# Retention, routed experts and a dense MLP: token rows turned by VectorE in 32x32 blocks instead of by TensorE

## The chip, the cores and the metric

The kernel runs on one core of a Trainium2 chip, in one launch. The metric is the device time of that launch in microseconds (us). Engines are named as the profile names them: PE is TensorE's matmuls and PEld its weight loads, DVE is VectorE, ACT ScalarE, POOL GpSimd, and SP the engine that issues most transfers. Each engine works through its own queue in program order.

## The reference

All inputs and outputs are fp32; the kernel has to keep fp32's precision.

```python
# 1: retention attention, 8 batches, 8 heads, 576 positions, 64 features
scores = scale * np.matmul(q, k.transpose(0, 1, 3, 2))
out = np.matmul(scores * Dmat[None], v)           # Dmat: decay by head, causal
x = out.transpose(0, 2, 1, 3).reshape(4608, 512)
# 2: each token goes to one of 8 experts
logits = x @ w_gate + modality_bias[modality_id]
e_idx = np.argmax(logits, axis=1)                 # gate_w: the softmax value there
h = np.maximum(x[mask] @ w1[e], 0.0)              # w1: 512 x 1024 for each expert
out[mask] = gate_w[mask, None] * (h @ w2[e])      # w2: 1024 x 512
# 3: dense MLP, 512 -> 2048 -> 512
h = x @ w_in
return (h - np.tanh(h)) @ w_out
```

## The kernel before

Three stages follow each other: attention and routing (up to about 161 us in the profile), the experts (to 609 us) and the dense MLP (to the end). An fp32 product is made of three matmuls: each operand is split into a high part, rounded to a format in which PE runs at full rate (a cast on ACT), and a low part, the rest (a subtraction on DVE); high x high, low x high and high x low are summed in PSUM.

**Expert units.** Routing sorts the tokens by expert into units of 400 (UE) of one expert each; twelve units are always run, u = 0 to 11. A unit has eight steps, f = 0 to 7, one for each 128 of the expert's 1024 hidden features. `blocks` (L647) writes the program: in step i come gemm1 (12 matmuls at L661, into the PSUM tile `hp`), then `post`, then `prep`, then gemm2 of the step two before (12 matmuls, L863 to L865, into four `acc` tiles of 128x400). At f=1 gemm2 finishes the unit before, and `finish` copies its four `acc` tiles to `yo`: two on ACT (L842), two on DVE (L840). The next gemm2, at f=2, starts the tiles anew, so it has to wait for these copies.

**post.** Relu on ACT gives `hi` (L760) and DVE gives `lo` (L761). Then the 512 columns of w2 for step i-1 and the 512 of w1 for step i+2 are each split: cast L736 on ACT, subtraction L737 on DVE. A transfer on SP's queue loads the step's weights for the next unit (`raw`).

**prep.** The rows of unit u+1 come from DRAM with four indirect transfers on POOL (L156), 128 rows of 512 floats each. They have tokens on the partitions, and gemm1 needs features there: at f=3 to 6 `turn_rows` has PE transpose one row tile in four pieces of 128x128 (L146) into an `hp` tile, ACT casts it (`xh`, L147) and DVE subtracts (`xl`, L148). For unit 1, this is done at (0,6) and (0,7); a pair (u,f) stands for step f of unit u.

**Conversion pieces.** The third stage's weights, stored as 64-bit floats, are converted to fp32 and split during the experts: 32 conversions of 128x512 (`conv`), each cut into four pieces: L174 to L177, then L181, then L185 and L186 with the cast L187 on ACT, then L191, all else on DVE. `prep` takes two pieces at even f and one at odd f from a list.

Around this, in code that is printed here:

Of the kernel before, what the change touches and what calls it, by code (L numbers as in the profile page):

```python
# [50 lines left out]


# [941 lines left out]
```

## Time and profile before

| | |
|---|---|
| median of 3 runs (lowest, highest) | 1391.44 us (1391.1, 1391.64) |
| the profiled execution, and its span | 1399.9 us, 1398.2 us |
| mean granted clock of PE | 0.998 |
| busy: PE, PEld, DVE, ACT, POOL | 99%, 86%, 75%, 50%, 16% |
| first and last matmul of gemm1 in the experts | 161.1 us, 600.5 us |
| first matmul of the dense MLP | 608.9 us |

The profiled execution is one of its own and is some 8 us longer than the runs without a profile. Busy shares are over the whole span. Times in the rows below are microseconds from the span's start, unless marked ns.

### The profile page before, as it was taken

Reading aid. Unit: us, or ns where it says so; the run is one execution under the profiler, and the core shown is the slowest. Engines: PE = TensorE matmul, PEld = TensorE weight load, DVE = VectorE, ACT = ScalarE, POOL = GpSimd, SP = SyncE. Lnnn points to the kernel's source line nnn. Section 1 sums busy time; section 2 is a strip of 40 time slices with the busy share of each in tenths; the row PEclk is TensorE's granted clock in tenths of the full one; section 3 lists DMA queues with packets and bytes.
Section 4 is the critical chain, followed back from the end, with each engine's and each line's share of the span. In section 5 each row is a group of like instructions: output and inputs, shape, how many; then the busy total and the mean of one; then the engine's idle time right before and its main releaser. Section 6 shows DMA issues by size and latency. Waiting matters only on the chain.

```text
span 1398.2 us, 22551 instructions
## 1 busy us (share of the span) xinstructions
PE 1377.8 (99%) x8427; PEld 1204.7 (86%) x8427; DVE 1045.4 (75%) x1762; ACT 693.6 (50%) x1302; POOL 220.9 (16%) x290
## 2 busy tenths in 40 slices
PE   8999899999999999999999999999999999999998
PEld 7887699999999999988888888888888888888886
DVE  5766578888888888658877777787787877778775
ACT  3323344444444444446656555565555655555553
POOL 4555320111111111010111100111001110011101
PEclk9999999999999999999999999999999999999999
DMA  9997444554854436434000000000000000000000
GB/s 369 407 338 271 149 143 138 138 126 124 222 140 93 93 86 168 123 129 153 31 31 31 31 1 30 31 31 31 1 30 31 31 31 0 31 31 0 31 0 31
DMA packets 65266, 136.50 MB, mean 98 GB/s; under 512 B 22656, under 2 KB 29376, under 8 KB 65152
## 3 DMA queue, kind: packets, MB, share of 16 engines
q1 hardware_dynamic: 50368, 96.77, 23.1%
q0 software_dynamic: 7296, 19.57, 4.1%
q10 hardware_dynamic: 7488, 18.67, 3.5%
q8 instruction: 68, 1.11, 0.3%
q14 instruction: 46, 0.38, 0.1%
HBM read 132.95 MB, written 39.80 MB: 124 GB/s over the span
## 4 chain that ended last, share of the span: by engine, by line
PE 51%; issue 5%; POOL 0%; POOLq 0%; ACT 0%; DVE 0%
PE hp L661 26%; PE acc L940 8%; PE acc L938 8%; PE acc L939 8%; POOL out_dram L964 0%; POOLq L990 0%; ACT o L961 0%; POOL nopt L963 0%; POOLq L954 0%; DVE epsb L969 0%; POOLq L964 0%; DVE epsb L968 0%
## 5 line engine op out<-in xcount | busy, mean ns | idle before, releaser
L911 ACT ACTIVATE eh<-hp 128x512 f32<-128x512 f32 x144 | 86.4, 600 | 294.7 <-PE hp L661 269.6
L661 PE MATMUL hp<-xh,winh 128*128 128x512 f32 x576 | 224.1, 389 | 1.6 <-DVE epsb L969 1.6
L938 PE MATMUL acc<-wout,hi 128*128 128x512 f32 x576 | 224.2, 389 | 0.0
L940 PE MATMUL acc<-wout,lo 128*128 128x512 f32 x576 | 224.2, 389 | 0.0
L939 PE MATMUL acc<-wout,hi 128*128 128x512 f32 x576 | 224.1, 389 | 0.0
L661 PE MATMUL hp<-xl,winh 128*128 128x512 f32 x576 | 224.1, 389 | 0.0
L661 PE MATMUL hp<-xh,winl 128*128 128x512 f32 x576 | 224.1, 389 | 0.0
L913 DVE TENSOR_TENSOR el<-eh,hp 128x512 f32<-128x512 f32 x144 | 99.1, 688 | 152.3 <-ACT eh L912 151.3
L922 DVE SCALAR_TENSOR_TENSOR el<-eh,el 128x512 f32<-128x512 f32 x144 | 128.5, 893 | 15.4 <-issue 0.5
L863 PE MATMUL acc<-hi,wh 128*128 128x400 f32 x384 | 136.1, 354 | 0.2
L661 PE MATMUL hp<-xh,wh 128*128 128x400 f32 x384 | 132.0, 344 | 1.8 <-ACT wh L736 1.8
L661 PE MATMUL hp<-xl,wh 128*128 128x400 f32 x384 | 131.7, 343 | 0.5 <-DVE xl L148 0.5
L661 PE MATMUL hp<-xh,wl 128*128 128x400 f32 x384 | 131.9, 343 | 0.1
L864 PE MATMUL acc<-lo,wh 128*128 128x400 f32 x384 | 131.4, 342 | 0.0
L865 PE MATMUL acc<-hi,wl 128*128 128x400 f32 x384 | 131.4, 342 | 0.0
L661 PEld LDWEIGHTS hp<-xh,winh 128*128 128x128 f32 x576 | 108.0, 188 | 24.1 <-PEq L884 1.9
L760 ACT ACTIVATE hi<-hp 128x400 fp32r<-128x400 f32 x96 | 48.5, 505 | 161.0 <-PE hp L661 161.0
L938 PEld LDWEIGHTS acc<-wout,hi 128*128 128x128 f32 x576 | 108.2, 188 | 22.8 <-ACT hi L916 0.4
L940 PEld LDWEIGHTS acc<-wout,lo 128*128 128x128 f32 x576 | 108.1, 188 | 22.9 <-DVE lo L917 0.4
L661 PEld LDWEIGHTS hp<-xl,winh 128*128 128x128 f32 x576 | 108.1, 188 | 22.6
L661 PEld LDWEIGHTS hp<-xh,winl 128*128 128x128 f32 x576 | 108.1, 188 | 22.4
L939 PEld LDWEIGHTS acc<-wout,hi 128*128 128x128 f32 x576 | 108.1, 188 | 22.4
(166 smaller groups left out, 2529.0 us busy)
## 6 DMA issues: line engine op xcount, KB each, us to landing
raw<-in_w_dram SPq DMA_DIRECT2D x91, 512.0 KB
qk<-in_qk_dram SPq DMA_DIRECT2D x36, 512.0 KB
vk<-in_vk_dram SPq DMA_DIRECT2D x36, 512.0 KB
y_d<-yo SPq DMA_DIRECT2D x12, 800.0 KB
yr<-y_d SPq DMA_DIRECT2D x9, 1024.0 KB
raw<-in_wo_dram SPq DMA_DIRECT2D x16, 512.0 KB
wo_d<-cv_em ACTq DMA_DIRECT2D x16, 512.0 KB
raw<-in_wi_dram SPq DMA_DIRECT2D x16, 512.0 KB
```

The lines of the kernel that those rows point to most:

```text
L661: nc.tensor.matmul(out=hp, lhsT=lhs, rhs=rhs, start=j == 0, stop=j == 3 * KD - 1)
L760: nc.scalar.activation(out=hi, in_=hp, func=ACTF.Relu)
L863: nc.tensor.matmul(out=o, lhsT=wh[:, cs], rhs=hi, start=first, stop=False)
L864: nc.tensor.matmul(out=o, lhsT=wh[:, cs], rhs=lo, start=False, stop=False)
L865: nc.tensor.matmul(out=o, lhsT=wl[:, cs], rhs=hi, start=False, stop=last)
L911: nc.scalar.activation(out=u, in_=hp, func=ACTF.Square)
L913: nc.vector.tensor_tensor(out=v, in0=u, in1=hp, op=ALU.mult)
L922: nc.vector.scalar_tensor_tensor(out=v, in0=s, scalar=SQ_C, in1=v, op0=ALU.add, op1=ALU.mult)
L938: nc.tensor.matmul(out=acc[s], lhsT=hi, rhs=wh, start=first, stop=False)
L939: nc.tensor.matmul(out=acc[s], lhsT=hi, rhs=wl, start=False, stop=False)
L940: nc.tensor.matmul(out=acc[s], lhsT=lo, rhs=wh, start=False, stop=last)
```

## The change

- **Rows of units 2 to 11.** `x_d` is stored with each row's 512 features in another order (`save_x`), so that a quarter of a row (128 floats) is a row of its own for the gather. A unit takes 13 indirect transfers of 128 quarters (L194) instead of four, with ids loaded by four transfers instead of one; both are issued one unit earlier, at (u-2, 4) and (u-2, 7). DVE turns the 32x32 blocks in place (`turn_blocks`, L169, at f=2 to 5: three of 128x512, one of 128x128), ACT casts (`split_high`, L182, at f=2 to 5) and DVE subtracts one step later (`split_low`, L186, at f=3 to 6). PE's transposes stay for unit 1 only. The expert weights lie twice in DRAM, with w1's rows in either order. Unit 2's weights are loaded unconditionally.
- **Weight splits.** One cast of 128x1024 (L791) and one subtraction of 128x1024 (L792) a step.
- **Conversion pieces.** The pieces are now L221 to L223; L227 and L228; L232 and L235 with ACT's cast L236; L240. They are doled out by a credit: a step earns 222 (RATE), each piece has a price (COST), a block transpose and its subtraction cost 69 each (TURN), and after a piece with a cast a step takes no more.
- **Output copies.** All four are on ACT (L913).

```diff
+UX = NB * QB
+TOK = NQ
+TURNED = 2
 UMIN = -(-NT // UE)
 UMAX = (NT - E) // UE + E
 CAP = NT
@@ -50,6 +56,11 @@
 NB3 = NT // UB
 
 
+TINY = 2.0 ** -15
+COST = 126, 111, 138, 69
+TURN = 69, 69
+RATE = 222
+
...
+    w1 = inputs["moe_w1"][:, FEATURES].reshape(E, KD, NQ, QB, F1, 128)
+    w1 = np.stack([w1.transpose(0, 4, 1, 3, 2, 5), w1.transpose(0, 4, 2, 3, 1, 5)], axis=2).reshape(E, F1, 2, 128, DM)
...
+        def turn_blocks(u, s, src):
+
+            b0, b1 = s * NQ, min(NB, s * NQ + NQ)
+            sq = src[:, b0:b1].rearrange("p i c -> p (i c)")
+            nc.vector.transpose(out=sq, in_=sq)
+
+        def blocks_of(u, s, src):
+            b0, b1 = s * NQ, min(NB, s * NQ + NQ)
+            w = min(QB, UE - b0 * QB)
+            c = slice(b0 * QB, min(b1 * QB, UE))
+            xf = src[:, b0:b1].rearrange("p i (k t) -> p k i t", k=KD)[:, :, :, 0:w]
+            return xf, [x[:, :, c].rearrange("p k (i t) -> p k i t", t=w) for x in xT[u]]
+
+        def split_high(u, s, src):
+            if s == 0:
+                new_xT(u)
+            xf, (xh, xl) = blocks_of(u, s, src)
+            nc.scalar.copy(out=xh, in_=xf)
+
+        def split_low(u, s, src):
+            xf, (xh, xl) = blocks_of(u, s, src)
+            nc.vector.tensor_tensor(out=xl, in0=xf, in1=xh.bitcast(F32), op=ALU.subtract)
+
+        def load_parts(base, idt):
+            with nc.allow_non_contiguous_dma(reason="one id per partition and block"):
+                for q in range(NQ):
+                    nc.sync.dma_start(out=idt[q * QB:(q + 1) * QB], in_=slot_d[bass.ds(base, UX), q:q + 1].rearrange("(i p) o -> p (i o)", p=QB))
+
+        def gather_parts(i, idt, dst):
+            nc.gpsimd.indirect_dma_start(out=dst, out_offset=None, in_=x_d[0:NT, :].rearrange("t (q c) -> (t q) c", q=NQ),
+                                         in_offset=bass.IndirectOffsetOnAxis(ap=idt[:, i:i + 1], axis=0))
+
         def load_ids(base, idt):
             with nc.allow_non_contiguous_dma(reason="one id per partition and tile"):
...
-                hi, a, e, m = d["raw"][:, :, 1], d["a"], d["e"], d["m"]
-                nc.vector.tensor_scalar(out=a, in0=hi, scalar1=3, scalar2=0x3FFFFFF8, op0=ALU.logical_shift_left, op1=ALU.bitwise_and)
+                hi, a, m = d["raw"][:, :, 1], d["a"], d["m"]
+                nc.vector.tensor_scalar(out=m, in0=hi, scalar1=0x7FFFFFFF, scalar2=None, op0=ALU.bitwise_and)
+                nc.vector.tensor_scalar(out=m.bitcast(F32), in0=m.bitcast(F32), scalar1=TINY, scalar2=None, op0=ALU.max)
+                nc.vector.tensor_scalar(out=a, in0=m, scalar1=3, scalar2=0x3FFFFFF8, op0=ALU.logical_shift_left, op1=ALU.bitwise_and)
+
+            def p2():
+                hi, a, e = d["raw"][:, :, 1], d["a"], d["e"]
                 nc.vector.scalar_tensor_tensor(out=a, in0=hi, scalar=-0x40000000, in1=a, op0=ALU.bitwise_and, op1=ALU.bitwise_or)
-                nc.vector.tensor_scalar(out=m, in0=hi, scalar1=0x7FFFFFFF, scalar2=None, op0=ALU.bitwise_and)
                 nc.vector.tensor_scalar(out=e, in0=a, scalar1=-0x800000, scalar2=None, op0=ALU.bitwise_and)
 
-            def p2():
+            def p3():
                 lo, e = d["raw"][:, :, 0], d["e"]
                 nc.vector.scalar_tensor_tensor(out=e.bitcast(F32), in0=lo.bitcast(U32), scalar=2.0 ** -52, in1=e.bitcast(F32), op0=ALU.mult, op1=ALU.mult)
 
-            def p3():
                 af, ef = (d[n].bitcast(F32) for n in "ae")
                 nc.vector.tensor_tensor(out=af, in0=af, in1=ef, op=ALU.add)
-                nc.vector.scalar_tensor_tensor(out=af, in0=d["m"], scalar=float(0x38100000), in1=af, op0=ALU.is_ge, op1=ALU.mult)
                 nc.scalar.copy(out=high(), in_=af)
 
             def p4():
@@ -197,7 +246,7 @@
                 if dst is not None:
                     nc.scalar.dma_start(out=dst, in_=d["em"].bitcast(F32))
 
-            return load, [lambda: (p0(), p1()), p2, p3, p4], save
+            return load, [(COST[0], lambda: (p0(), p1())), (COST[1], p2), (COST[2], p3), (COST[3], p4)], save
...
             def save_x(t, tp, spare):
-                xo = P["xg"].tile([128, DM], F32, name="xg") if spare else xo_p.tile([128, DM], F32, name="xo")
-                nc.scalar.mul(out=xo, in_=tp.rearrange("p k t -> p (k t)"), mul=gate[:, t:t + 1])
+                xo = xo_p.tile([128, DM], F32, name="xo")
+                nc.scalar.mul(out=xo.rearrange("p (q k m) -> p k q m", q=NQ, k=KD),
+                              in_=tp.rearrange("p k (q m) -> p k q m", q=NQ), mul=gate[:, t:t + 1])
...
+                def split_w(*parts):
+                    parts = sorted((2 * (i % F1) + half, i, half) for i, half in parts if 0 <= i < len(steps))
+                    if parts:
+                        n, j = len(parts), parts[0][0]
+                        r = raw[:, j:parts[-1][0] + 1:max(parts[-1][0] - j, 1)]
+                        wh, wl = (w_p.tile([128, 2, DM], F32R, name=n) for n in ("wh", "wl"))
+                        nc.scalar.copy(out=wh[:, 0:n], in_=r)
+                        nc.vector.tensor_tensor(out=wl[:, 0:n], in0=r, in1=wh[:, 0:n].bitcast(F32), op=ALU.subtract)
+                        for k, (_, i, half) in enumerate(parts):
+                            wsp[i, half] = (wh[:, k], wl[:, k])
...
                     hi, lo = (ht_p.tile([128, UL], F32R, name=n)[:, 0:UE] for n in ("hi", "lo"))
                     nc.scalar.activation(out=hi, in_=hp, func=ACTF.Relu)
                     nc.vector.scalar_tensor_tensor(out=lo, in0=hp, scalar=0.0, in1=hi.bitcast(F32), op0=ALU.max, op1=ALU.subtract)
                     ht[i] = (hi, lo)
+                    split_w((i - 1, 1), (i + 2, 0))
                     if i > 0:
-                        split_w(i - 1, 1)
                         load_raw(i - 1 + F1)
-                        raws.pop(i - 1)
-                    split_w(i + 2, 0)
...
+                    for v, g in ((1, 2), *((v, 4) for v in range(TURNED, UMIN))):
+                        if (u, f) == (max(v - 2, 0), g):
+                            idts[v] = ids_of(v)
+                        if (u, f) == ((0, 3) if v == 1 else (v - 2, F1 - 1)):
+                            gather(v, idts.pop(v))
+                    if u == 0 and f >= 6:
+                        for s in range(2 * f - 12, 2 * f - 10):
+                            tr_x(1, s)
+                    credit[0] += RATE if u > 0 or f > 4 else 0
+                    if 0 < u < UMIN - 1:
+                        v = u + 1
+                        if f in range(3, 3 + SE):
+                            split_low(v, f - 3, xg[v])
+                            credit[0] -= TURN[1]
+                        if f in range(2, 2 + SE):
+                            turn_blocks(v, f - 2, xg[v])
+                            split_high(v, f - 2, xg[v])
+                            credit[0] -= TURN[0]
...
-                    for _ in range(2 - f % 2 if u > 0 or f > 4 else 0):
-                        if fill2:
-                            fill2.pop()()
+                    while fill2 and fill2[-1][0] <= credit[0]:
+                        c, piece = fill2.pop()
+                        credit[0] -= c
+                        piece()
+                        if c == COST[2]:
+                            break
 
                 def finish(u, acc):
                     yo = P["yo"].tile([128, 4, UE], F32, name="yo")
                     for c in range(4):
-                        if c % 2:
-                            nc.vector.tensor_copy(out=yo[:, c], in_=acc[c][:, 0:UE])
-                        else:
-                            nc.scalar.copy(out=yo[:, c], in_=acc[c][:, 0:UE])
+                        nc.scalar.copy(out=yo[:, c], in_=acc[c][:, 0:UE])
```

At (3,1), ACT's queue: Relu, weight cast, the conversion's cast and the copies of unit 2's output. Before:

```order
L760 ACTIVATE hi<-hp 128x400
L736 CAST wh_4051<-raw_2548 128x512
L736 CAST wh_4074<-raw_2583 128x512
L187 CAST cv_em<-cv_a 128x512
L842 COPY yo<-acc 128x400 x2
```

After:

```order
L824 ACTIVATE hi<-hp 128x400
L791 CAST wh<-raw 128x1024
L236 CAST cv_em<-cv_a 128x512
L247 DMA wo_d<-cv_em 128x1024
L913 COPY yo<-acc 128x400 x4
```

All four copies now stand behind the cast `cv_em<-cv_a`. In the same step on DVE, before:

```order
L761 SCALAR_TENSOR_TENSOR lo<-hp,hi 128x400
L737 TENSOR_TENSOR wl_4052<-raw_2548,wh_4051 128x512
L737 TENSOR_TENSOR wl_4075<-raw_2583,wh_4074 128x512
L185 TENSOR_TENSOR cv_a<-cv_a,cv_em 128x512
L186 SCALAR_TENSOR_TENSOR cv_a<-cv_em,cv_a 128x512
L840 COPY yo<-acc 128x400 x2
```

After:

```order
L825 SCALAR_TENSOR_TENSOR lo<-hp,hi 128x400
L792 TENSOR_TENSOR wl<-raw,wh 128x1024
L227 SCALAR_TENSOR_TENSOR cv_a<-raw,cv_a 128x512
L228 TENSOR_SCALAR cv_em<-cv_a 128x512
L232 SCALAR_TENSOR_TENSOR cv_em<-raw,cv_em 128x512
L235 TENSOR_TENSOR cv_a<-cv_a,cv_em 128x512
```

Four conversion instructions stand where two stood, ahead of the one that ACT's cast reads (L235), and no copies follow. At (2,4) and the start of (2,5), DVE's queue before (`xl<-hp` reads the rows that PE has turned):

```order
L761 SCALAR_TENSOR_TENSOR lo<-hp,hi 128x400
L737 TENSOR_TENSOR wl_3802<-raw_2583,wh_3801 128x512
L737 TENSOR_TENSOR wl_3807<-raw_2649,wh_3806 128x512
L148 TENSOR_TENSOR xl<-hp,xh 128x4x128
L185 TENSOR_TENSOR cv_a<-cv_a,cv_em 128x512
L186 SCALAR_TENSOR_TENSOR cv_a<-cv_em,cv_a 128x512
L191 TENSOR_TENSOR cv_em<-cv_a,cv_em 128x512
```

After:

```order
L825 SCALAR_TENSOR_TENSOR lo<-hp,hi 128x400
L792 TENSOR_TENSOR wl<-raw,wh 128x1024
L186 TENSOR_TENSOR xl<-xg,xh 128x4x128
L169 STREAM_TRANSPOSE xg<-xg 128x512
L232 SCALAR_TENSOR_TENSOR cv_em<-raw,cv_em 128x512
L235 TENSOR_TENSOR cv_a<-cv_a,cv_em 128x512
```

The subtraction of the rows now comes from `xg`, a block transpose follows it, and then two conversion instructions. On ACT at (2,4), before:

```order
L760 ACTIVATE hi<-hp 128x400
L736 CAST wh_3801<-raw_2583 128x512
L736 CAST wh_3806<-raw_2649 128x512
L147 CAST xh<-hp 128x4x128
L187 CAST cv_em<-cv_a 128x512
```

After:

```order
L824 ACTIVATE hi<-hp 128x400
L791 CAST wh<-raw 128x1024
L182 CAST xh<-xg 128x4x128
L236 CAST cv_em<-cv_a 128x512
L247 DMA wo_d<-cv_em 128x1024
```

The cast of the rows (L182) reads what DVE has just turned, and stands with L236 between the weight cast and what comes next, Relu.

## Rows read from the trace of the kernel before

**Rows 1.** The profile's page, busy time, share and instructions of each engine.
```profile
PE 1377.8 (99%) x8427; PEld 1204.7 (86%) x8427; DVE 1045.4 (75%) x1762; ACT 693.6 (50%) x1302; POOL 220.9 (16%) x290
```

**Rows 2.** Timeline of PE in unit 5: start, us, then the instruction.
```profile
347.70 0.34 PE L661 MATMUL hp<-xh,wh 128*128 128x400 f32 x1
...
354.18 0.34 PE L863 MATMUL acc<-hi,wh 128*128 128x400 f32 x1
...
356.34 0.34 PE L661 MATMUL hp<-xh,wh 128*128 128x400 f32 x1
...
358.32 0.34 PE L661 MATMUL hp<-xh,wl 128*128 128x400 f32 x1
358.68 0.42 PE L863 MATMUL acc<-hi,wh 128*128 128x400 f32 x1
...
360.93 0.34 PE L661 MATMUL hp<-xh,wh 128*128 128x400 f32 x1
...
363.09 0.60 PE L146 MATMUL hp<-ident,xg 128*128 128x128 f32 x4
...
380.11 0.34 PE L661 MATMUL hp<-xh,wh 128*128 128x400 f32 x1
```

**Rows 3.** Windows of units 1 to 10 (199.86 to 568.05): sum and mean.
```profile
sum 368.19, PE 367.53 PEld 359.86 DVE 300.78 ACT 161.88 POOL 40.84; mean PE 36.75 PEld 35.99 DVE 30.08 ACT 16.19 POOL 4.08
```

**Rows 4.** Timeline of ACT and DVE at unit 5's f=1: start, us, instruction.
```profile
354.38 0.51 ACT L760 ACTIVATE hi<-hp 128x400 fp32r<-128x400 f32 x1 [2.79 <-PE hp L661]
...
354.78 1.13 ACT L736 CAST wh<-raw 128x512 fp32r<-128x512 f32 x2
...
354.92 0.57 DVE L761 SCALAR_TENSOR_TENSOR lo<-hp,hi 128x400 fp32r<-128x400 f32 x1
...
355.42 1.30 DVE L737 TENSOR_TENSOR wl<-raw,wh 128x512 fp32r<-128x512 f32 x2
...
356.63 0.69 DVE L185 TENSOR_TENSOR cv_a<-cv_a,cv_em 128x512 f32<-128x512 f32 x1
...
357.36 0.69 DVE L186 SCALAR_TENSOR_TENSOR cv_a<-cv_em,cv_a 128x512 f32<-128x512 int32 x1
...
357.96 1.05 DVE L840 COPY yo<-acc 128x400 f32<-128x400 f32 x2
358.08 0.62 ACT L187 CAST cv_em<-cv_a 128x512 fp32r<-128x512 f32 x1 [2.17 <-DVE cv_a L186]
...
358.61 0.88 ACT L842 COPY yo<-acc 128x400 f32<-128x400 f32 x2
```

**Rows 5.** Lines L147, L148, L174 (ns min/median/max), and the page's row of L922.
```profile
L147 ACT CAST xh<-hp x44: 213/588/601, 193.0 to 562.7; 128x512 fp32r<-128x512 f32 x33, 128x64 fp32r<-128x64 f32 x11
...
L148 DVE TENSOR_TENSOR xl<-hp,xh x44: 215/684/689, 193.8 to 563.5; 128x512 fp32r<-128x512 f32 x33, 128x64 fp32r<-128x64 f32 x11
...
  PE hp L661: 0.5, 1
...
L174 DVE TENSOR_SCALAR cv_a<-raw x32: 414/420/442, 189.5 to 572.7; 128x512 int32<-128x512 int32 x32
...
L922 DVE SCALAR_TENSOR_TENSOR el<-eh,el 128x512 f32<-128x512 f32 x144 | 128.5, 893 | 15.4 <-issue 0.5
```

**Rows 6.** Line L156, the gathers: ns min/median/max, and idle time before them.
```profile
L156 POOL DMA_INDIRECT xg<-x_d,idt x44: 852/949/1475, 184.1 to 543.4; - x44
...
  issue: 10.7, 35
```

**Rows 7.** Windows: us, busy us of PE, PEld, DVE, ACT, POOL, then granted clock.
```profile
159.30:161.10 1.80, 0.01 (x1) 0.01 (x1) 1.35 (x3) 1.80 (x6) 0.00 (x0) 1.00 0.47 189
163.00:166.00 3.00, 3.00 (x12) 2.87 (x12) 0.43 (x1) 0.96 (x2) 0.00 (x0) 0.50 0.00 0
607.00:609.00 2.00, 0.44 (x3) 0.14 (x3) 0.69 (x3) 0.34 (x1) 0.00 (x0) 1.00 0.02 4
609.00:612.00 3.00, 3.00 (x14) 2.48 (x15) 0.00 (x0) 0.08 (x1) 0.00 (x0) 1.00 0.85 278
```

More of the change, by code (lines that the diff above doesn't have):

```diff
@@ L37 @@
 PAD = 224
+QB = 32
+NQ = TL // QB
+NB = -(-UE // QB)
+UX = NB * QB
+TOK = NQ
+TURNED = 2
 UMIN = -(-NT // UE)
@@ L134, with new_xT @@
         xT, P = {}, {}
+        def new_xT(u):
+            p = xT_p[1 if u == "t" else u % 2]
+            xT[u] = [p.tile([128, KD, UB if p is xT_p[0] else UL], F32R, name=n)[:, :, 0:UE] for n in ("xh", "xl")]
         def turn_rows(u, s, src, tp):
             if s == 0:
-                p = xT_p[1 if u == "t" else u % 2]
-                xT[u] = [p.tile([128, KD, UB if p is xT_p[0] else UL], F32R, name=n)[:, :, 0:UE] for n in ("xh", "xl")]
+                new_xT(u)
             xh, xl = xT[u]
@@ L495 @@
             nc.gpsimd.iota(tokid, pattern=[[TL, NTILE], [0, SW]], base=0, channel_multiplier=1)
+            nc.gpsimd.iota(tokid[:, :, 0:NQ], pattern=[[NQ * TL, NTILE], [1, NQ]], base=0, channel_multiplier=NQ)
             nc.gpsimd.iota(mio, pattern=[[0, E], [UE, ncap]], base=0, channel_multiplier=0,
@@ L724, in load_raw @@
                         u, f = steps[i]
-                        cond = {"cond": val(u, 3), "cond_hint": False} if u != "t" and u > 0 else {}
-                        raws[i] = raw_p.tile([128, 2 * DM], F32, name=f"raw{f}") if i < F1 else raw_of.pop(i - F1)
-                        raw_of[i] = raws[i]
+                        cond = {"cond": val(u, 3), "cond_hint": False} if u not in ("t", 0, TURNED) else {}
                         eng, w = (nc.scalar, first_act) if u == 0 and f > 2 else (nc.sync, val(u, 1))
-                        eng.dma_start(out=raws[i], in_=A["w12"][bass.ds(w, 1), f].rearrange("o p c -> (o p) c"), **cond)
@@ L731, in split_w @@
-                def split_w(i, half):
-                    if i < len(steps):
-                        r = raws[i][:, half * DM:(half + 1) * DM]
-                        wh = w_p.tile([128, DM], F32R, name=f"wh{half}")
-                        wl = w_p.tile([128, DM], F32R, name=f"wl{half}")
-                        nc.scalar.copy(out=wh, in_=r)
-                        nc.vector.tensor_tensor(out=wl, in0=r, in1=wh.bitcast(F32), op=ALU.subtract)
-                        wsp[i, half] = (wh, wl)
@@ L743, in ids_of @@
+                def ids_of(u):
+                    if by_blocks(u):
+                        idt = P["id"].tile([128, NB], I32, name="idt")
+                        load_parts(val(u, 0), idt)
+                    else:
+                        idt = P["id"].tile([128, SE], I32, name="idr")
+                        load_ids(val(u, 0), idt)
                     return idt
                 def gather(u, idt):
-                    xg[u] = []
-                    for s in range(SE):
-                        t = P["xg"].tile([128, DM], F32, name="xg")
-                        gather_rows(s, idt, t)
-                        xg[u].append(t)
+                    t = P["xg"].tile([128, SE * DM], F32, name="xg")
+                    if by_blocks(u):
+                        xg[u] = t[:, 0:NB * 128].rearrange("p (i c) -> p i c", c=128)
+                        for i in range(NB):
+                            gather_parts(i, idt, xg[u][:, i])
+                    else:
+                        xg[u] = t.rearrange("p (s c) -> p s c", c=DM)
+                        for s in range(SE):
+                            gather_rows(s, idt, xg[u][:, s])
@@ L787, in swap @@
                     P["acc"] = po("acc", 4, space=PSUM, side="right")
-                    P["id"] = pr("id2", 2, side="right")
+                    P["id"] = pr("id2", 1, side="right")
                     P["yo"] = pr("yo2", 1, side="right")
```

50 lines of the change are left out of this document (23 added, 27 removed).

## The prediction, made before the changed kernel was run

> **What bounds the kernel now.** I read the page first: PE is busy for 1377.8 of 1398.2 us [rows 1], so a stretch gets shorter only if PE has less to do or waits less. Next comes PE's timeline of one expert unit, unit 5 [rows 2]. Two steps without extras, 347.70 to 356.34, take 8.64 us: 4.32 a step, 24 matmuls of 0.18. Step f=2 (356.34 to 360.93) takes 4.59: 0.27 more, because gemm1 ends issuing at 358.32 + 0.18 = 358.50 and gemm2's first matmul starts at 358.68 and is drawn out. Steps f=3 to 6 (360.93 to 380.11) take 19.18 instead of 4 x 4.32 = 17.28: 1.90 us for the transposes that begin at 363.09. The windows of units 1 to 10 say that this is the pattern: 368.19 us for ten, PE busy for 367.53 of them, DVE for 30.08 of the 36.82 of each [rows 3]. Last I read DVE and ACT at the end of f=1, where the output copies stand [rows 4]: they are queues in program order that hand work to each other, and the conversion's cast at 358.08 starts 2.17 us after ACT was free, when DVE's L186 is done. The copies behind it release PE.
>
> **What the change takes away.** The transposes of ten units (2 to 11): 10 x 1.90 = 19.0 us [rows 2]. If the f=2 waits went too, 11 x 0.27 = 3.0 more: together 22.0.
>
> **Prices of the new work.** The merged cast: 128x512 takes 0.588 and 128x64 0.213 on ACT, so 0.84 ns a column, and 1024 columns 1.05 (two casts now take 1.13 with their overlap). The merged subtraction: 0.684 and 0.215 on DVE give 1.05 ns a column and 1.22 for 1024 (two take 1.30) [rows 4, 5]. A conversion is now three instructions like L174 (0.42), one of 0.69, one of 0.42, two of 0.69, ACT's cast of 0.62, and a last 0.69 [rows 4, 5]: 4.4 us on DVE, as before. No row shows a block transpose. It is between 0.42, a one-source 128x512 in SBUF, and 0.89, the dearest mean of a DVE 128x512 [rows 5]; I take 0.69, what most 128x512 instructions cost, since the ends are equally far. The splits of the rows, 0.62 on ACT and 0.69 on DVE, replace those that read PSUM at 0.588 and 0.684 [rows 5]. The Trainium skill (VectorE: DVE Perf Modes, The three transpose paths) puts a 128x128 bf16 block transpose on VectorE at 311 ns, faster than TensorE's; as an estimate from it, with 384 columns more at 1.05 ns, 128x512 would take 0.71 us, which leaves the sum as it is. No row of this trace shows it.
>
> DVE's sum stays under PE's: 8 x (0.57 + 1.22) for lo and weights, 2.76 conversions (32 [rows 5] over 11.6 units) x 4.43, and 3 transposes with their splits and a small one (4.5) are 31.0 us of 34.56. But the order decides, since a wait on ACT or DVE holds all behind it.
>
> **Cost 1: the copies at f=1.** Count from gemm2's first matmul (354.18 in unit 5 [rows 2]); the next gemm2 is due at 4.32 and needs its wl at 4.68. By the rows, Relu starts at 0.20, the cast at 0.60 (to 1.65), lo runs 0.74 to 1.31, the subtraction 1.68 to 2.90. A dependent DVE instruction starts some 0.04 later, an independent one 0.08 earlier, than its forerunner ends [rows 4]. In step (3,1) the order has four conversion instructions then: 2.82 to 3.51, 3.55 to 3.97, 4.01 to 4.70, 4.74 to 5.43. The cast follows, 5.46 to 6.08, and only then the copies, all four on ACT: the first ends at 6.49. PE followed the first copy by 0.15 (357.96 + 0.57 to 358.68 [rows 4, 2]), so it waits until 6.64: 2.3 us. Before, two copies were on DVE, which needed no cast. And (2,7) ends with the same four instructions, so its cast delays the next Relu from 4.52 to 5.99, (3,0)'s lo and weights follow late, four more instructions end 1.92 into (3,1), the copy at 7.21: a wait of 3.0. Units 2, 6, 10 and 11 have two conversion instructions at f=1, but six ahead of them at f=0, and a cast at (u-1,7): copy at 5.95, wait 1.78 (1.50 if nothing is late from the unit before). Unit 7 is like them, but follows a (6,6) with five conversion instructions; I take it as unit 3. Units 1, 4, 5, 8 and 9 have no cast at f=1 and wait for nothing. Sum: 2 x 3.0 + 4 x 1.78 = 13.1; without lateness 2.3 + 5 x 1.50 = 9.8; if all eleven waited, 19.6.
>
> **Cost 2: f=2 to 6.** There each step is a ring: subtraction 1.22, L186 0.69, transpose 0.69, ACT's cast of the rows (L182) 0.62, Relu 0.51, weight cast 1.05, and again the subtraction. Those add to 4.78; with 0.28 of net overlap at the handovers the ring is 4.5 us, over 4.32: what is late stays late. In unit 2 the copies end 1.1 into (2,2), Relu follows them, the subtraction ends at 3.8, and transpose and six conversion instructions at 7.5, 3.2 into (2,3), whose own subtraction ends at 4.8: PE waits 0.15 for wl, and by the ring 0.15 again in (2,4). Behind (2,4)'s subtraction two conversion instructions and their cast enter the ring (0.69 + 0.69 + 0.62): (2,5)'s Relu starts at 3.5 instead of 2.1 and its wl is there at 6.2, 1.5 late. Together 1.8 for unit 2. Units 6 and 10 have a cast inside the ring too: 1.8. Units 1 and 5 have it one step earlier with more slack: 1.3. For 3, 4, 7, 8 and 9, between nothing and 2.0, I take the middle, 1.0. Sum: 3 x 1.8 + 2 x 1.3 + 5 x 1.0 = 13.0. Ends: 1 (if lateness is not carried) and 10 x 1.8 = 18.
>
> **Cost 3: unit 0.** (0,6) holds four conversion instructions (2.5 us) behind the row splits, and PE already waits 0.5 for xl there [rows 5]. I add 1.0, between 0 and 1.7.
>
> **At nothing:** the thirteen gathers a unit (POOL is busy for 4.08 of 36.82 us [rows 3]; uncovered, rival D), the id loads and unit 2's eight unconditional weight loads (on SP's queue, a unit ahead), and the third stage, whose matmuls don't change.
>
> **The sum:** -22.0 + 13.1 + 13.0 + 1.0 = +5.1 us on the profiled execution's 1399.9. The median of the runs is 8.5 below that execution, so 1391.4 + 5.1 = **1396.5 us**. With all ends low -22.0 + 9.8 + 1 = -11.2, with all high -22.0 + 19.6 + 18 + 1.7 = +17.3.
>
> **Rivals.**
> A, the other side: lateness isn't carried, because ACT and DVE have slack in steps without a cast (ACT is busy for 16.19 of 36.82 us [rows 3]) and the ring comes out below 4.32 (a transpose of 0.42 alone makes it 4.23). Then only f=1's copies wait: -11.2, **1380.2**. It decides if the ring is shorter than a step.
> B: DVE's sum, 31.0 of 34.56, decides and order doesn't: -22 to -19, **1370 to 1372**. Against it: the copies stand behind the cast in ACT's queue whatever the sum, and in [rows 4] a copy waited for just that.
> C: block transposes and strided splits are dear. At 0.89 for the transpose and both splits the ring grows by 0.67 in three steps of ten units: +20, **1416**.
> D: gathers come late. POOL takes 0.949 + 0.30 for each, 16.2 us for 13; the first four are due 13.0 us (three steps) after their issue, the last 25.9 after. At the longest seen, 1.475 + 0.30 [rows 6], and 3 us late, the twelfth ends at 24.3 where 21.6 is due: 2.7 a unit, +27 on the forecast, **1424**. The Trainium skill (SBUF — State Buffer, the trap "DVE blocks DMA") has it that a transfer issued by GpSimd can't have its descriptors written while VectorE holds the shared port, and gives 620 ns against some 3100. By that the gathers would be late everywhere; the trace of before, whose longest is 1.475 with DVE busy for 82% of a unit, doesn't bear it out.
> E: PE's clock. After a wait of 1.80 us (159.3 to 161.1) the granted clock was 0.50 for the 3 us from 163: 1.5 lost; after about 1.6 us idle at 607 to 609 it stayed at 1.00 [rows 7]. If each of the six waits of 1.78 and more costs 1.5, that is +9: **1405**. It lies inside the range.
>
> **Chances.** The forecast 0.54 (of it 0.06 are E); A 0.25; B 0.08; C 0.09; D 0.04. A measurement of this kernel tells about 0.2%, 2.8 us, from no change. Faster: A 0.24, B 0.08, the forecast's low end 0.02: 0.34. Same: 0.01 of A and 0.08 of the forecast: 0.09. Slower: the other 0.44 of the forecast, C and D: 0.57. The range 1379 to 1410 goes from A to the sum with all ends high and leaves out B, C and D: 0.21. The forecast's own range is 1388 to 1410.
>
> **What would show it.** Right: no PE transposes in units 2 to 11; steps f=3 to 6 near 17.3 us in units 3, 4, 7, 8; PE waiting at the start of f=2 for ACT's copies, 2 to 3 us in units 3 and 7, 1.5 to 2 in 2, 6, 10, 11, little in the others; a wait of 1 to 2 us for wl at f=4 to 6 in units 2, 6 and 10; casts of 1.05 and subtractions of 1.22. Wrong: a unit mean at or below 34.9; block transposes below 0.42 or above 0.9; copies that end before PE needs them; PE or DVE waiting for gathers.

## The result, and the profile after

The changed kernel takes 1406.55 us (median of 4 runs, 1405.18 to 1408.08) where the kernel before takes 1391.54 on the same chip: a ratio of 1.0109 (95% interval 1.0097 to 1.0122), slower by 15 us. The profiled execution took 1405.85 us with a span of 1404.1.

The page's first line, beside [rows 1]: PE is busy for 13 us less, and yet the span is longer.

```profile
PE 1364.6 (97%) x8267; PEld 1190.4 (85%) x8267; DVE 1053.9 (75%) x1685; ACT 697.2 (50%) x1233; POOL 324.8 (23%) x381
```

The windows of the changed kernel up to its first expert matmul, and from there to the first matmul of the dense MLP (columns as in [rows 7]):

```profile
0.00:153.76 153.76, 145.65 (x2453) 119.22 (x2453) 99.30 (x245) 50.28 (x116) 81.77 (x131) 1.00 0.89 328
153.76:614.80 461.04, 434.79 (x2359) 422.27 (x2359) 356.94 (x575) 201.07 (x331) 159.56 (x147) 0.99 0.51 138
```

The experts take 461.04 us; in the profile of before it was 447.8 (161.1 to 608.9, in the table above). So 13.2 of the 15 us are lost there. The two spans differ by 5.9 only: in the profile of before the first stage is some 7 us longer, and experiment 1 finds the same on a chip on which that kernel takes 1399.4 us (median of 7 runs), profiled or not. So profiling doesn't make a run 8 us longer; the profile of before most likely comes from such a chip.

What PE waited for in the experts, some of the rows (total us, times, longest):

```profile
PE acc L934 <- ACT yo L913: 16.7, 6, 3.7
PE acc L936 <- DVE wl L792: 3.7, 7, 0.8
...
PE acc L934 <- ACT wh L791: 0.5, 2, 0.3
```

Before, no such row had more than 2 us in the experts. In unit 2, the timeline of DVE, ACT and PE around the end of f=1 (f=1's gemm2 began at 236.5, the next was due at 240.8), which answers to [rows 4]:

```profile
237.82 0.43 DVE L221 TENSOR_SCALAR cv_em<-raw 128x512 int32<-128x512 int32 x1 [1.72 <-DMA wo_d<-cv_em]
...
239.34 0.74 DVE L227 SCALAR_TENSOR_TENSOR cv_a<-raw,cv_a 128x512 int32<-128x512 int32 x1
...
240.12 0.43 DVE L228 TENSOR_SCALAR cv_em<-cv_a 128x512 int32<-128x512 int32 x1
...
240.48 0.56 DVE L825 SCALAR_TENSOR_TENSOR lo<-hp,hi 128x400 fp32r<-128x400 f32 x1
...
240.96 1.21 DVE L792 TENSOR_TENSOR wl<-raw,wh 128x1024 fp32r<-128x1024 f32 x1
...
242.09 0.68 DVE L232 SCALAR_TENSOR_TENSOR cv_em<-raw,cv_em 128x512 f32<-128x512 uint32 x1
...
242.80 0.69 DVE L235 TENSOR_TENSOR cv_a<-cv_a,cv_em 128x512 f32<-128x512 f32 x1
...
243.53 0.62 ACT L236 CAST cv_em<-cv_a 128x512 fp32r<-128x512 f32 x1 [5.39 <-DVE cv_a L235]
...
244.05 1.67 ACT L913 COPY yo<-acc 128x400 f32<-128x400 f32 x4
...
244.59 0.45 PE L934 MATMUL acc<-hi,wh 128*128 128x400 f32 x1 [3.60 <-ACT yo L913]
```

DVE stands still for 1.72 us before L221: the buffer `cv_em` that it is to write is still being read by the store of the conversion two before. Everything behind it is late by that much, then the two conversion instructions of f=1 (L232, L235) follow, the cast at 243.53, and only then the copies. PE waits 3.60 us. What PE does next is slow. Here are windows of unit 2 before, in and after the wait, and after the waits of units 6 and 11:

```profile
238.00:240.00 2.00, 2.00 (x13) 2.00 (x12) 1.90 (x4) 0.14 (x1) 1.70 (x2) 1.00 1.00 381
242.00:244.00 2.00, 0.00 (x0) 0.00 (x0) 1.46 (x3) 0.47 (x1) 1.70 (x2) 1.00 0.26 66
244.60:248.40 3.80, 3.80 (x12) 3.76 (x13) 1.89 (x3) 2.46 (x5) 2.83 (x3) 0.55 0.48 167
395.00:398.80 3.80, 3.80 (x13) 3.76 (x14) 2.00 (x3) 2.34 (x5) 2.88 (x4) 0.55 0.47 156
582.50:586.30 3.80, 3.80 (x14) 3.77 (x13) 2.62 (x4) 1.72 (x3) 0.00 (x0) 0.55 0.67 223
```

The granted clock is 0.55 over the 3.8 us in which the next 12 matmuls run: most of it at half clock, 1.20 GHz instead of 2.40. By their starts (244.59 to gemm1's 248.43) they take 3.84 us instead of 2.16: 1.7 lost, in units 2 and 6 alike. In unit 11, after a wait of 2.3 us, the same 1.7 are lost, 1.1 in gemm2 and 0.6 in the next gemm1. After waits of 2.9, 2.5 and 1.6 us in units 3, 7 and 10 the clock stayed up.

The durations of the new instructions (ns, min/median/max), beside [rows 5, 6]:

```profile
L169 DVE STREAM_TRANSPOSE xg<-xg x40: 302/703/707, 208.3 to 562.7; 128x512 f32<-128x512 f32 x30, 128x128 f32<-128x128 f32 x10
...
L182 ACT CAST xh<-xg x40: 244/621/626, 209.1 to 563.0; 128x512 fp32r<-128x512 f32 x30, 128x64 fp32r<-128x64 f32 x10
...
L186 DVE TENSOR_TENSOR xl<-xg,xh x40: 216/684/687, 214.7 to 565.8; 128x512 fp32r<-128x512 f32 x30, 128x64 fp32r<-128x64 f32 x10
...
L791 ACT CAST wh<-raw x99: 610/1039/1092, 153.1 to 608.3; 128x1024 fp32r<-128x1024 f32 x93, 128x512 fp32r<-128x512 f32 x6
...
L792 DVE TENSOR_TENSOR wl<-raw,wh x99: 677/1225/1285, 153.7 to 608.9; 128x1024 fp32r<-128x1024 f32 x93, 128x512 fp32r<-128x512 f32 x6
...
L194 POOL DMA_INDIRECT xg<-x_d,idt x130: 938/947/1778, 189.7 to 550.4; - x130
```

For all units at once, the same reading as in [rows 2]: the time from each step's first gemm1 matmul to the next one's, less 4.32 us. This difference is called the excess. The upper row of a kernel is the excess at f=2, the lower one that of the other seven steps (of before: the transposes, 1.9). The numbers 4 to 9 are those of the experiments below.

| excess, us, in unit | 1 | 2 | 3 | 4 | 5 | 6 | 7 | 8 | 9 | 10 | 11 | sum |
|---|---|---|---|---|---|---|---|---|---|---|---|---|
| before, f=2 | 0.3 | 0.3 | 0.3 | 0.2 | 0.3 | 0.3 | 0.3 | 0.3 | 0.3 | 0.3 | 0.3 | 3.0 |
| before, others | 2.8 | 1.9 | 1.9 | 1.9 | 1.9 | 1.9 | 1.9 | 1.9 | 1.9 | 1.9 | 0.0 | 19.9 |
| after, f=2 | 0.0 | 5.4 | 3.2 | 0.0 | 0.6 | 5.6 | 2.8 | 0.0 | 0.3 | 1.9 | 3.6 | 23.4 |
| after, others | 3.0 | 0.1 | 0.2 | 0.5 | 1.8 | 0.3 | 0.3 | 0.5 | 2.0 | 1.9 | 1.7 | 12.2 |
| 4, shared copies, f=2 | 1.7 | 5.6 | 2.8 | 1.6 | 2.3 | 2.7 | 3.1 | 1.6 | 4.2 | 1.4 | 3.7 | 30.7 |
| 6, copies first, f=2 | 0.0 | 2.6 | 0.0 | 0.0 | 0.5 | 1.0 | 0.1 | 0.0 | 0.3 | 0.0 | 0.0 | 4.4 |
| 6, others | 4.0 | 2.5 | 2.5 | 0.5 | 1.8 | 2.8 | 1.4 | 0.5 | 2.0 | 8.3 | 3.5 | 29.8 |
| 8, PE turns, f=2 | 0.0 | 2.1 | 4.4 | 0.0 | 0.0 | 1.7 | 1.7 | 0.0 | 0.0 | 1.7 | 1.7 | 13.4 |
| 9, cast late, f=2 | 0.0 | 0.0 | 0.0 | 0.0 | 0.0 | 0.0 | 0.0 | 0.0 | 0.0 | 0.0 | 0.0 | 0.0 |
| 9, others | 0.6 | 0.4 | 0.0 | 0.0 | 0.0 | 0.0 | 0.0 | 0.0 | 0.0 | 0.0 | 0.9 | 2.0 |

After against before: 23.4 - 3.0 at f=2 and 12.2 - 19.9 elsewhere are +12.7 of the 13.2; 0.5 more lies behind unit 11's last step.

### The profile page after: what moved, and what is told of

Read it like the earlier page. It is cut to its first block, busy times and chain, and to the rows that moved or that the text cites. A ratio compares the mean times of both kernels' runs of the same rounds, so it can differ in the third digit from the quotient of the medians.

```text
span 1404.1 us, 22247 instructions
## 1 busy us (share of the span) xinstructions
PE 1364.6 (97%) x8267; PEld 1190.4 (85%) x8267; DVE 1053.9 (75%) x1685; ACT 697.2 (50%) x1233; POOL 324.8 (23%) x381
## 3 DMA queue, kind: packets, MB, share of 16 engines
q1 hardware_dynamic: 63520, 101.01, 23.4%
## 4 chain that ended last, share of the span: by engine, by line
PE 50%; issue 5%; POOL 0%; POOLq 0%; ACT 0%
PE hp L712 26%; PE acc L1013 8%; PE acc L1012 8%; PE acc L1011 8%; POOL out_dram L1037 0%; POOLq L1063 0%; ACT o L1034 0%; POOL nopt L1036 0%; POOLq L1027 0%; POOLq L1037 0%
## 5 line engine op out<-in xcount | busy, mean ns | idle before, releaser
L194 POOL DMA_INDIRECT xg<-x_d,idt x130 | 144.1, 1108 | 226.5 <-DVE cv_em L232 39.2
L740 POOL TENSOR_TENSOR xl<-yr,xh 128x512 fp32r<-128x512 f32 x36 | 49.2, 1365 | 441.7 <-ACT xh L739 441.7
L936 PE MATMUL acc<-hi,wl 128*128 128x400 f32 x384 | 135.9, 354 | 3.9 <-DVE wl L792 3.7
L792 DVE TENSOR_TENSOR wl<-raw,wh 128x1024 fp32r<-128x1024 f32 (+1 forms) x99 | 118.8, 1200 | 24.1 <-ACT wh L791 23.1
L1011 PEld LDWEIGHTS acc<-wout,hi 128*128 128x128 f32 x576 | 108.3, 188 | 22.7 <-ACT hi L989 0.4
```

The costliest lines, as they stand in the source:

```text
L194: nc.gpsimd.indirect_dma_start(out=dst, out_offset=None, in_=x_d[0:NT, :].rearrange("t (q c) -> (t q) c", q=NQ), in_offset=bass.IndirectOf ...
L792: nc.vector.tensor_tensor(out=wl[:, 0:n], in0=r, in1=wh[:, 0:n].bitcast(F32), op=ALU.subtract)
L936: nc.tensor.matmul(out=o, lhsT=wl[:, cs], rhs=hi, start=False, stop=last)
L1011: nc.tensor.matmul(out=acc[s], lhsT=hi, rhs=wh, start=first, stop=False)
```

## The experiments

The theory: instructions that wait for VectorE's conversion (ACT's cast L236) stand in ACT's queue ahead of work that PE waits for, the output copies at f=1 and the Relu of the next step at f=3 to 6. The rivals: VectorE simply has too much work; the block transposes themselves; late transfers. Experiments 1 to 4 ran on a chip where the kernel before takes 1399.4 us, 5 to 8 and 9 to 12 on others (1391.3, 1391.2); each ratio is to before on the same chip. The changed kernel was not run on the first of these, so 2 to 4 are compared with it across chips.

**1. The kernel before, again.** No edit.

> The kernel before once more, to see where its first profiled execution (1399.9 us) lost 8.5 us against the runs (1391.4). If the loss lay in the first stage, the first expert matmul, at 161.1 us there, now stands near 153.5, where the changed kernel has it (153.8), and the experts from there to the dense MLP take 447.8 us as before. If it lay elsewhere, that matmul stays at 161.

It took 1399.8 us, the other runs there 1399.4 (median of 7). Its windows up to the first expert matmul and through the experts:

```profile
0.00:160.82 160.82, 147.99 (x2454) 120.33 (x2454) 97.72 (x244) 50.28 (x117) 81.73 (x131) 1.00 0.86 316
160.82:608.70 447.88, 444.95 (x2518) 435.06 (x2518) 349.31 (x653) 197.40 (x400) 54.42 (x55) 1.00 0.51 131
```

The first stage takes 160.8 us again, and the experts 447.9. So this chip is slower in the first stage, and by these two numbers the profile of before came from such a one, which the record doesn't name. The experts take the same in both traces, which is why experts are compared across chips here.

**2. No conversion piece with a cast at f=1.**

```diff
-while fill2 and fill2[-1][0] <= credit[0]:
+while fill2 and fill2[-1][0] <= credit[0] and not (f == 1 and fill2[-1][0] == COST[2]):
```

> The changed kernel, but at f=1 no conversion piece with a cast is taken, so that it goes to f=2 instead. Theory (the copies behind the conversion's cast in ACT's queue): PE's waits at the start of f=2, 23.4 us of the changed kernel with their half-clock stretches, fall to 2 or less; steps f=2 to 6 take perhaps 3 us more; 1385 to 1390 us. Rival (VectorE has too much work and the lateness goes where it likes): the waits move to f=3 to 6, and the time stays above 1400.

1423.4 us, ratio 1.0181 (1.0163 to 1.0199): slower than the changed kernel's 1.0109. The excess at f=2 did fall, from 23.4 to 3.8 us in all, but that of the other steps grew to 34.8. In unit 10 two steps took 10.3 and 11.0 us; VectorE waited there for rows:

```profile
DVE xg L169 <- DMA xg<-x_d,idt: 7.1, 2, 6.9
```

The copies were where the theory had the loss, but its time was missed: the loss moved to other steps and to a transfer that had been covered by it. That is nearer to the rival, which had the waits move and the time stay above 1400. The trace is of the fastest of the four runs, 1417.7 us, and what the others lost beyond it isn't seen.

**3. Three buffers for `cv_em`.** `bufs=2` becomes 3.

> The changed kernel with three buffers instead of two for the converted weights (cv_em), so that L221 needn't wait for the store of the conversion two before. Theory: the two waits for that store (3.6 us together, in units 2 and 6) go, PE's waits there fall from 3.6 to below 2, and with them the clock may stay full: 3.6 to 7 us less, 1400 to 1403 us. Rival: the copies would be as late without that wait: 1406.

1412.4 us, ratio 1.0091 (1.0075 to 1.0108). No wait for the store is left in the trace. At f=2 PE waits 1.78 and 1.50 us in units 2 and 6 instead of 3.60 and 3.71, and the excess there is 3.6 (1.6 of it at half clock) and 1.8 instead of 5.4 and 5.6. But this trace is of the slowest of the five runs, 1422.0 us, which lost time elsewhere (f=2 in unit 3: 4.5, unit 6's other steps 4.5). The interval overlaps that of the changed kernel (1.0097 to 1.0122): by itself this edit is worth little, 2.5 us by the medians against 1.0109 and 5 against 1.0127 (experiment 5).

**4. Copies shared by ACT and VectorE.**

```diff
-nc.scalar.copy(out=yo[:, c], in_=acc[c][:, 0:UE])
+if c % 2:
+    nc.vector.tensor_copy(out=yo[:, c], in_=acc[c][:, 0:UE])
+else:
+    nc.scalar.copy(out=yo[:, c], in_=acc[c][:, 0:UE])
```

> The changed kernel with the output copies shared by ACT and VectorE as before. Theory: VectorE's first copy stands behind L235 only, not behind the cast, so PE's waits in units 2, 3, 6, 7, 10 and 11 get 0.6 to 0.7 us shorter each, and VectorE has 1.05 us more in each unit: 1401 to 1405 us. Rival (it is the cast alone): the waits go altogether, 1388.

1420.9 us, ratio 1.0151 (1.0134 to 1.0168): worse, a miss. PE now waits at f=2 in nearly all units, also in 1, 4 and 8 (table), and for VectorE's copy:

```profile
PE acc L937 <- DVE yo L914: 19.9, 9, 4.1
```

VectorE's copies stand behind all its conversion instructions of the step, cast or not. So moving the copies to ACT was not the mistake of the change. That it is what stands ahead of them is tested in 6 and 9.

**5. The changed kernel again.**

> The changed kernel itself, beside the others on the same chip. Ratio to before near 1.011 as measured; PE's waits at f=2 in units 2, 3, 6, 7, 10 and 11 as in its first trace (16.7 us for ACT's copies, and half-clock stretches after the longest).

1409.0 us, ratio 1.0127 (1.0110 to 1.0144); 463.0 us in the experts, 17.9 us of waits for the copies. The loss repeats.

**6. Copies ahead of the cast.** At f=1 the pieces are written behind the copies.

```diff
-piece()
+held.append(piece) if f == 1 and u > 0 else piece()
...
 yos[u] = yo
+while held:
+    held.pop(0)()
```

> The changed kernel, but at f=1 the conversion pieces are written after the output copies, so that ACT does the copies first and the conversion's cast behind them; VectorE's instructions and their order stay as they are. Theory (copies behind the cast): PE's waits at f=2 go in all units, with the half-clock stretches, 20 us or more; waits for wl at f=3 to 6 (11 us) stay: ratio 0.993 to 0.997, faster than before. Rival (VectorE's work, or late transfers, hold PE whatever the order on ACT): 1.004 or more, with waits for wl or rows in place of those for the copies.

1404.4 us, ratio 1.0081 (1.0062 to 1.0101). The excess at f=2 fell as the theory says, from 24.5 us in experiment 5 to 4.4, with the same instructions in the same order on VectorE. But the time fell by 4.6 us only, and the theory's ratio was missed: the other steps' excess rose from 13.5 to 29.8. PE's longest waits in the experts, and one of VectorE's:

```profile
PE acc L938 <- DVE wl L792: 12.0, 18, 2.0
PE acc L936 <- ACT wh L791: 3.7, 4, 2.9
...
DVE xg L169 <- DMA xg<-x_d,idt: 5.1, 2, 4.6
```

The rival's number was hit, though not its reason, as 9 shows. PE's long wait at f=2 had given VectorE and ACT time to catch up; without it their lateness shows at the next cast, in the steps f=2 to 6, and at the rows of unit 11.

**7. The same with three buffers for `cv_em`.**

> The same with three buffers for the converted weights. Theory: without the wait for the store (two waits, 3.6 us in the changed kernel) VectorE is less late in units 2 and 6: equal to the kernel without that edit or up to 4 us faster, ratio 0.991 to 0.997.

1397.4 us, ratio 1.0030 (1.0014 to 1.0046): 7 us faster than 6, more than the 4 of the theory, though its ratio wasn't reached. So the wait for the store does matter once the copies are out of the way. f=2 costs 1.3 us in all. What PE waits for now are weights, high and low; that they are late because of the casts ahead of them is shown by 9 only:

```profile
PE acc L938 <- DVE wl L792: 9.6, 15, 2.1
PE acc L936 <- ACT wh L791: 4.7, 6, 2.1
```

and, in unit 10, rows. The store of a unit, the last gather and the transpose that waits for it (start, us; in brackets idle time and releaser):

```profile
542.61 0.41 SPq L836 DMA_DIRECT2D y_d<-yo  x1
...
543.83 1.02 POOL L194 DMA_INDIRECT xg<-x_d,idt  x1 [0.30 <-issue]
...
558.64 0.31 DVE L169 STREAM_TRANSPOSE xg<-xg 128x128 f32<-128x128 f32 x1 [3.77 <-DMA xg<-x_d,idt]
```

The gather issued 1.2 us behind the 800 KB store is used 14.8 us after its issue, when the transpose at last may start; the median from issue to landing is 3.2 us in this run. That the store makes it late is not shown.

**8. PE turns the rows in all units.** Ids, gathers and `tr_x` for units 2 to 11 as in the kernel before; pieces in the same steps, merged splits, all copies on ACT.

```diff
-split_low(v, f - 3, xg[v])
+tr_x(v, f - 3)
...
-turn_blocks(v, f - 2, xg[v])
-split_high(v, f - 2, xg[v])
```

> The changed kernel with rows gathered whole and turned by PE in all units, as before; merged weight splits, conversion pieces in the same steps, and all copies on ACT stay. Theory: the waits at f=2 are made by the copies behind the cast and stay in units 2, 3, 6, 7, 10 and 11 (10 to 18 us with their half-clock stretches), the waits for wl at f=3 to 6 go, PE has its 19 us of transposes back: ratio 1.006 to 1.013. Rival (block transposes and their splits on VectorE make the loss): no waits at f=2, ratio 0.998 to 1.002.

1405.7 us, ratio 1.0104 (1.0087 to 1.0121), as the theory says. With no block transpose in these units, PE waits for copies

```profile
PE acc L933 <- ACT yo L912: 10.2, 6, 2.6
```

at f=2 in units 2, 3, 6, 7, 10 and 11 and in no other (table): exactly those with a cast at f=1. Unit 3's 4.4 us hold a half-clock stretch again, after a wait of 2.6 us (granted clock 0.50 from 282.5 to 284.5). The rival is out: the transposes don't make this wait.

**9. ACT's cast one step later.** The conversion's cast is written at the start of the next step's fill, behind that step's Relu and weight cast.

```diff
-nc.scalar.copy(out=high(), in_=af)
+owed.append(lambda: nc.scalar.copy(out=high(), in_=af))
...
 def p4():
+    while owed:
+        owed.pop()()
...
+while owed:
+    owed.pop()()
 credit[0] += RATE if u > 0 or f > 4 else 0
```

> The changed kernel, but ACT's cast of a conversion is written at the start of the next step's prep, behind that step's Relu and weight cast, so that neither the copies nor a Relu stand behind a cast that waits for VectorE's last instruction. VectorE's instructions and order stay. Theory (ACT's order makes both the waits for copies and those for wl): PE's waits at f=2 and those of 1 to 1.5 us for wl at f=3 to 6 go, about 25 of the 34 us that PE waits; what stays are the waits for transfers (the store of the conversion two before, the rows of unit 11): ratio 0.991 to 0.998. Rival (only the copies are held by ACT's order; wl is late because VectorE is): as the kernel with the copies first, 1.003 to 1.008.

1371.9 us, ratio 0.9868 (0.9851 to 0.9884): 35 to 37 us less than the changed kernel (1406.6 and 1409.0), and faster than before. That is more than the theory's number. Timeline at (3,1) and into (3,2):

```profile
269.56 0.51 ACT L828 ACTIVATE hi<-hp 128x400 fp32r<-128x400 f32 x1 [2.36 <-PE hp L716]
...
269.96 1.04 ACT L795 CAST wh<-raw 128x1024 fp32r<-128x1024 f32 x1
...
270.90 1.68 ACT L919 COPY yo<-acc 128x400 f32<-128x400 f32 x4
...
272.17 0.69 DVE L229 SCALAR_TENSOR_TENSOR cv_a<-raw,cv_a 128x512 int32<-128x512 int32 x1
...
272.89 0.43 DVE L230 TENSOR_SCALAR cv_em<-cv_a 128x512 int32<-128x512 int32 x1
...
273.36 0.74 DVE L234 SCALAR_TENSOR_TENSOR cv_em<-raw,cv_em 128x512 f32<-128x512 uint32 x1
...
273.68 0.34 PE L940 MATMUL acc<-hi,wh 128*128 128x400 f32 x1
...
273.88 0.51 ACT L828 ACTIVATE hi<-hp 128x400 fp32r<-128x400 f32 x1 [1.30 <-PE hp L716]
...
274.13 0.69 DVE L237 TENSOR_TENSOR cv_a<-cv_a,cv_em 128x512 f32<-128x512 f32 x1
...
275.22 0.62 ACT L238 CAST cv_em<-cv_a 128x512 fp32r<-128x512 f32 x1
```

The four conversion instructions are still there, and L237 still ends after PE's next gemm2 has begun, but the copies run from 270.90 and PE starts at 273.68, on time. The cast follows in the next step, at 275.22. The longest of PE's waits up to the first matmul of the dense MLP, which is the first row:

```profile
PE hp L716 <- PEq L963: 1.6, 1, 1.6
PE hp L716 <- ACT wh L795: 1.1, 1, 1.1
PE acc L942 <- DVE wl L796: 0.8, 2, 0.6
```

Units 3 to 10 take 34.56 us, 8 x 4.32 exactly. The waits for rows went, and those for wl but for 0.8 us: they were lateness made by the place of the casts in ACT's queue, since VectorE does the same work in the same order.

**10. With three buffers for `cv_em`.**

> The same with three buffers for the converted weights. Theory: the wait for the store goes: 2 to 5 us less than with the late cast alone, 0.989 to 0.995. Rival (the store's wait was covered): equal to the late cast alone.

1370.9 us, ratio 0.9851 (0.9835 to 0.9868). The medians are 1.0 us apart and the intervals overlap; the trace has 0.4 us less excess, in unit 2. That is the rival, or nearly: the store was covered.

**11. And gathers three steps earlier.** Four row buffers, so that a unit's gathers are issued at (u-2, 4) and its ids at (u-2, 1), from unit 3 on.

> The same again, with the rows in four buffers that come free one by one, so that the gathers of a unit are issued three steps earlier, at f=4 instead of f=7 two units ahead (ids at f=1). Theory (in the faster versions PE waits in unit 10 because the last gathers are issued beside the store of the unit before): no wait for rows, another 5 to 10 us less: ratio 0.985 to 0.990, faster than both kernels. Rival (the transfers of unit 11's rows are slow whenever they are issued): equal to the run before it.

1369.7 us, ratio 0.9846 (0.9829 to 0.9862): equal to 10, and not 5 to 10 us less. The theory missed: with nothing late, the rows come in time anyway.

**12. PE turns the rows, with the late cast.**

> PE turns the rows in all units as before, with the late cast. Theory: the waits at f=2 that this kernel had without the late cast (10.2 us and half-clock stretches) go, and with them 3 us that the kernel before has there: ratio 0.996 to 1.001. The difference to the late cast with early gathers is then what turning on VectorE is worth: 14 to 19 us. Rival (merged splits and the new pieces cost by themselves): 1.004 or more.

1390.5 us, ratio 0.9999 (0.9989 to 1.0008). No excess at f=2, and 1.9 us a unit for the transposes. Against 9, turning on VectorE is worth 1390.5 - 1371.9 = 18.6 us, against 11, which has earlier gathers and a third buffer too, 20.8. The trace is of the fastest of the ten runs, 1387.6 us; by the traces of 9 and 12 the excess of units 1 to 11 differs by 19.0, the prediction's number, and the experts as a whole by 16.5. The rival is out: with the late cast, and PE turning the rows, the kernel takes what it took before, so merged splits and the new conversion pieces cost at most the 3 us that f=2 gave back.

## Why the prediction came out as it did

The direction was right, the way too; the sum (+5.1) was short by 10. Cost 1 came out 10.3 above its term and Cost 2 3.8 below; unit 11 behind f=2 (1.7) and the stretch behind its last step (0.5) had no term; unit 0 gave 0.4 instead of 1.0; and 1.8 lie outside the experts. That the time fell inside the range is in part luck, since errors of opposite sign partly cancel.

- **Removed work**, -19.0 and -3.0: right. In 12 the transposes cost 1.9 in each of ten units, in 9 nothing, and f=2 has no excess in either.
- **Prices**: block transpose 0.70 us (0.69 taken), merged cast 1.04 (1.05), subtraction 1.23 (1.22), L182 0.62 (0.62), L186 0.68 (0.69). All hit. The estimate of 0.71 us for the block transpose, worked out from the 311 ns for 128x128 bf16 of the Trainium skill (VectorE: DVE Perf Modes, The three transpose paths), agrees with the trace at 128x512; for fp32 128x128 the trace has 0.30.
- **Cost 1**, copies at f=1: right in its place (units 2, 3, 6, 7, 10, 11; nothing in 1, 4 and 8) and its cause (experiments 6, 8, 9), mis-sized: 13.1 forecast, 23.4 measured. Units 3, 7 and 10 have 3.2, 2.8 and 1.9 for 3.0, 3.0 and 1.8. Units 2 and 6 have 5.4 and 5.6 for 1.8: 1.7 of it is the half clock, and about 1.8 the wait for the store of `cv_em` (1.72 and 1.86 on VectorE), which the prediction did not have. Without that wait, in experiment 3, PE waits 1.78 and 1.50 there, the two numbers that the prediction worked out. Unit 11 has 3.6, of it 1.1 of half clock, and the wait is 0.7 longer than forecast: it follows a (10,6) with five conversion instructions, as unit 7 follows (6,6). The clock was rival E, put inside the forecast but not in the sum; it came in three of the six waits.
- **Cost 2**, f=2 to 6: a ring of 4.5 us was forecast, and lagging steps take 4.46 to 4.49 (units 1, 5, 9 and 10). The sum was 13.0; units 1 to 10 have 9.2 (the table's 12.2 less 1.7 in unit 11 and 1.3 at (1,0)). Units 1, 5 and 10 have 1.6, 1.8 and 1.9 for 1.3, 1.3 and 1.8. Units 2 and 6 have 0.1 and 0.3 for 1.8, for the long wait at f=2 let VectorE catch up: in experiment 7, where that wait is gone, they have 2.2 and 2.0. Of the five taken at the middle, 1.0, unit 9 has 2.0 and the others 0.2 to 0.5. Experiment 9 shows the cause: with the conversion's casts out of the way it is gone.
- **Cost 3**: the steps (0,6) to (1,0) have an excess of 4.1 us instead of 2.9, in both traces of either kernel: 1.2, where 1.0 was forecast. The sum shows 0.4 of it, because unit 0's first steps happen to be 0.8 shorter than in the profile of before.
- **At nothing**: right for the gathers of the changed kernel, where no row shows a wait for them. It was cover, not absence: in 2, 6 and 7 the last rows of unit 11 were waited for. Wrong for the end of unit 11: the third stage's preparation on GpSimd meets VectorE there (last section), and (11,6) lost 1.1 us.
- **Rivals**: A (lateness not carried) is out; C too, by the durations of the transposes and splits; D's waits didn't come, though 23 of the 130 gathers took 1.4 to 1.8 us, most of them longer than the 1.475 that D was worked out from. B's time, 1370 to 1372, is what experiment 9 reaches: VectorE's work does fit, once ACT's order lets it. That B failed for the reason given against it is shown by 9.

Left open: why a half-clock stretch followed some waits and not others, and the last 1.8 us of the 15, which lie outside the experts, where the two profiles come from chips that differ.

## What to carry to other kernels

In ACT's queue here, an instruction that waited for VectorE's last result held everything behind it. Write such a hand-over where its input is long done, a step later, behind the work that others wait for: here that one edit turned +1.1% into -1.3%. Fixing one wait alone may show little (experiment 6), as the lateness moves to the next place where the same hand-over stands; look for all places of the pattern before judging the whole change.
